# Spreading the kernel values of a long convolution: a second 0/1 matrix in place of a shifted copy, and new instruction orders

## The chip, the cores and the metric

The kernel runs on one core of one Trainium2 chip. The metric is device time in microseconds (us) of one execution; before the change it is 368.26 us, the median of three runs (367.65 to 368.64). A core has a matrix engine (TensorE, PE in the profile), a vector engine (VectorE, DVE), a scalar engine (ScalarE, ACT), GpSimd (POOL) and SyncE (SP, here used to start transfers). Each engine works through its own list of instructions in order; where one needs what another made, it waits on a semaphore.

## The reference

Two independent computations share one output of 2048 x 1280 bf16. The left half is attention with 32 heads of 20 columns, in which position s sees the eight positions s, s-2, ..., s-14. The right half is a long convolution: a kernel of 2048 taps for each of 640 channels is summed from 192 complex exponentials, and convolved with the input through Fourier transforms.

```python
idx = pos[:, None] - (jnp.arange(8) * 2)[None, :]          # left half
logits = einsum("bhsd,bhswd->bhsw", q, k[idx]) * scale      # masked where idx < 0
a = einsum("bhsw,bhswd->bhsd", softmax(logits), v[idx]) @ wo
...
l = arange(L).astype(bf16)                                  # right half: positions rounded to bf16
P = exp((dt * (A_re + 1j * A_im))[:, :, None] * l)
K = einsum("dn,dnl,dn->dl", Cc, P, dt * Bc).real            # 640 x 2048 taps
y = irfft(rfft(u, 2L) * rfft(K, 2L))[:L] + u * Dskip
```

Because the positions are rounded to bf16, the 2048 taps take far fewer distinct values: the kernel computes K for 20 offsets times 33 blocks of 8 positions, and a 0/1 matrix spreads these over the 2048 positions.

## The kernel before

**Stages.** The convolution goes through five chunks c = 0 to 4 of 128 channels. For each chunk VectorE builds two tables from powers that ScalarE made: Xtab, 20 offsets (stage xtab), and Ytab, 33 blocks (ypos for blocks 16 to 32, yneg for 0 to 15, the latter with the magnitudes of stage mag). There are two Xtab buffers, but one Ytab: ypos of the next chunk can begin only when the table products of this one have been read from Ytab. Its generators come from device memory by SyncE (taby, five transfers a chunk), and GpSimd zeroes the first block (line 546).

**Table products.** Stage kgen (two halves h of a chunk, kgen30 and kgen31 for chunk 3) multiplies the tables, channel by channel, 33 columns at a time, into two PSUM banks: 16 zeroing matmuls, 256 narrow ones with 64 rows (line 603) and 256 wide ones (line 610) for a chunk, each with its own weight load. A half was three pieces on PE: `both` (zeroing and all narrow products) and `one` twice. ScalarE then copies each bank into Kd (line 615).

**Shift and spreading.** Kd has 20 rows of each 32-row group in use. Positions that need block b + 1 where their neighbours need b take it from rows 20 to 31 of the group, into which four SyncE transfers a chunk (stage kd, line 583) copied rows 4 to 15, moved by one block. Spreading (stage spread, its first four pieces, line 635) multiplies Kd by the 0/1 matrix SEL into K; the next eight pieces are the first Fourier step of K (f1, line 656). Stage u is the same step for the input. spec is the second Fourier step (f2, line 676, copied to Sp at line 681), prod the product of both spectra on VectorE (lines 686 and 687), swap a copy of one spectrum with its halves exchanged, inv the first inverse step (ia, line 701, copied at line 704). last00 to last07 and last10 to last13 are the second inverse step, from tables HB that take the place of Xtab, Xg, krtmp and mag when those are done (stage hb, six loads). uda and udb are the input times Dskip, loaded where Xtab0 and Ytab were.

**Attention.** k0 to v3 are the projections (line 745). For each of four blocks b of 512 positions, logits has ten VectorE products (line 791), five PE pieces that sum them (line 798), then maximum, exponential and normalisation; av has ten VectorE products with v (line 840) and ten PE pieces (line 848); out is the output projection (line 865) with writes by SyncE (line 870). fetch and fetchv load q, k and v for a block. The products go through three buffers (pr), so VectorE can be at most three products ahead of PE.

**The order of work.** It is written out in lists. Every stage registers its pieces by engine (`op("P", ...)` for PE, A for ScalarE, V for VectorE, G for GpSimd, S for SyncE). TRACE lists all pieces in the order in which they are emitted, SLOTS gives the buffer of every use of the eight PSUM banks (ps) and of other shared buffers, and SEQ gives each engine's own order, which `chain` fixes by dependencies without waits:

```python
for ins in next(left[stage, engine]):
    if engine in last:
        self.tc.add_manual_dep(ins, last[engine].name, ...)
    last[engine] = ins
```

A word "kgen30.P:2" in SEQ is the next two PE pieces of stage kgen30.

## Time and profile before

| | |
|---|---|
| median of three runs | 368.26 us (367.65 to 368.64) |
| profiled execution | 368.48 us, of which the span from first to last instruction is 366.7 |
| busy: DVE, PE, ACT, POOL | 306.6, 281.9, 257.1, 35.2 us |
| mean granted PE clock | 0.900 |
| spreading, line 635 | 180 matmuls, 7.0 us busy |
| shift, line 583 | 20 issues on SP, 24 KB each, median 0.83 us |
| table products, lines 603 and 610 | 1280 matmuls each, 14.6 and 26.9 us busy |

Times in the profile are of one execution, counted from its first instruction. A row of stretches gives the stretch, its length, then for each engine the busy time with the number of instructions, then the granted share of the PE clock, the DMA engines' busy share and GB/s. In a timeline or a list of waits, "[5.51 <-PE ps_l L798]" says that the engine was idle 5.51 us before that instruction, until the named one had finished; "issue" is idle time in which it waited for nothing that the profile shows.

### The profile page before, as it was taken

What the parts mean: (1) busy time and instruction counts of PE and PEld (TensorE: products, weight loads), DVE (VectorE), ACT (ScalarE), POOL (GpSimd) and SP (SyncE); (2) the same over time, 40 slices, a digit from 0 to 9 for tenths busy, and PEclk for the clock granted to TensorE, in tenths of its full rate; (3) what the DMA queues carried; (4) which work ended last, traced back from release to release, by engine and by line L of the source; (5) the groups of instructions that cost most, each with busy time, mean ns of one, the idle gap of its engine ahead of it and who ended that gap; (6) DMA issues with size and microseconds to landing.
All of it is one profiled execution on the core that took longest, in us unless ns stands there. A gap on an engine that the chain in (4) does not pass through costs nothing.

```text
span 366.7 us, 13345 instructions
## 1 busy us (share of the span) xinstructions
PE 281.9 (77%) x5808; PEld 183.3 (50%) x5808; DVE 306.6 (84%) x397; ACT 257.1 (70%) x574; POOL 35.2 (10%) x72
## 2 busy tenths in 40 slices
PE   2429999999945787849985579869886569899983
PEld 1213434443333454637663456647565356768852
DVE  1588999999997999999999879999999259979620
ACT  3998999964530679926897048945997029999663
POOL 9550000000000000000000000000000000002282
PEclk9999999999975988958999558979999589999999
DMA  6998869897997789811739614564998689998695
GB/s 142 226 123 198 215 224 308 269 291 221 251 260 168 183 108 170 158 46 44 208 72 170 185 41 154 105 61 141 245 327 258 222 153 121 160 192 233 154 202 136
DMA packets 127114, 65.49 MB, mean 179 GB/s; under 512 B 84352, under 2 KB 123872, under 8 KB 125904
## 3 DMA queue, kind: packets, MB, share of 16 engines
q1 hardware_dynamic: 124224, 61.61, 72.7%
q0 software_dynamic: 1776, 2.79, 3.9%
q8 instruction: 45, 0.74, 0.9%
q10 hardware_dynamic: 1056, 0.25, 0.3%
q14 instruction: 13, 0.11, 0.1%
HBM read 35.25 MB, written 21.03 MB: 153 GB/s over the span
## 4 chain that ended last, share of the span: by engine, by line
PE 27%; DVE 20%; ACT 17%; issue 14%; DMA 13%; SPq 7%; ACTq 0%; DVEq 0%
PE ps_k L610 6%; ACT A L660 4%; SPq L724 4%; PE ps_k L603 4%; DVE p L840 3%; PE ps_f L676 3%; PE ps_o L848 3%; DMA out_dram<-ob 3%; ACT Sp L681 3%; PE ps_op L865 2%; DMA UT<-Sp 2%; DMA xT<-in_A_x_dram 2%; DVE prod L791 2%; ACT am L464 2%; PE ps_l L798 2%
## 5 line engine op out<-in xcount | busy, mean ns | idle before, releaser
L745 PE MATMUL ps_p<-xT,w 128*128 128x512 bf16 x300 | 68.8, 386 | 5.6 <-DMA xT<-in_A_x_dram 4.0
L791 DVE TENSOR_TENSOR prod<-qk 128x2048 bf16<-128x2048 bf16 x40 | 48.5, 1238 | 12.8 <-PE ps_l L798 12.0
L840 DVE TENSOR_TENSOR p<-vb,attn 128x2048 bf16<-128x2048 bf16 x40 | 47.5, 1225 | 10.3 <-PE ps_o L848 8.5
L745 PEld LDWEIGHTS <-w 128*128 128x128 bf16 x300 | 29.1, 98 | 44.2 <-issue 11.7
L681 ACT CAST Sp<-ps_f 128x512 bf16<-128x512 f32 (+1 forms) x96 | 44.8, 560 | 8.8 <-PE ps_f L676 8.3
L615 ACT CAST Kd<-ps_k 128x264 bf16<-128x264 f32 x20 | 7.7, 387 | 60.0 <-PE ps_k L610 60.0
L660 ACT CAST A<-ps_f 128x512 bf16<-128x512 f32 x80 | 45.7, 692 | 0.4 <-PE ps_f L656 0.4
L610 PE MATMUL ps_k<-Ytab,Xtab 128*20 128x33 bf16 x1280 | 26.9, 250 | 21.1 <-issue 21.0
L610 PEld LDWEIGHTS <-Xtab 128*20 128x20 bf16 x1280 | 23.6, 127 | 25.3 <-issue 24.7
L748 ACT CAST st<-ps_p 128x512 bf16<-128x512 f32 x60 | 31.6, 611 | 6.4 <-PE ps_p L745 4.0
L676 PE MATMUL ps_f<-A,cT 64*128 64x128 bf16 (+1 forms) x768 | 29.6, 222 | 6.1 <-issue 2.2
L676 PEld LDWEIGHTS <-cT 64*128 64x128 bf16 x768 | 22.7, 102 | 16.7 <-issue 15.6
L848 PE MATMUL ps_o<-p,cHs 64*32 64x256 bf16 x640 | 25.5, 306 | 3.3 <-DVE p L840 2.0
L556 ACT ACTIVATE mag<-ta 128x192 bf16<-128x192 f32 x80 | 24.6, 415 | 3.3 <-DVE Ytab L561 3.2
L865 PE MATMUL ps_op<-wo,oT 128*128 128x320 bf16 x160 | 24.6, 300 | 0.4 <-ACT A L660 0.4
L603 PE MATMUL ps_k<-Ytab,Xtab 64*20 64x33 bf16 x1280 | 14.6, 241 | 11.8 <-issue 11.8
L1138 POOL DMA_DIRECT2D out_dram<-ys x24 | 14.4, 608 | 95.7 <-ACT Sp L681 80.5
L546 POOL MEMSET Ytab<- 128x192 bf16 x5 | 1.3, 258 | 221.7 <-PE ps_k L610 221.7
L701 PE MATMUL ps_ia<-cE,Sp 128*128 128x128 bf16 x160 | 19.7, 219 | 2.8 <-DVE Sp L687 2.5
L509 DVE TENSOR_TENSOR krtmp<-Xtab,Xg 128x3072 bf16<-128x3072 bf16 (+1 forms) x15 | 20.5, 1368 | 0.3
L798 PE MATMUL ps_l<-prod,cGs 128*32 128x512 bf16 x160 | 17.0, 446 | 3.8 <-DVE prod L791 3.5
L603 PEld LDWEIGHTS <-Xtab 64*20 64x20 bf16 x1280 | 13.4, 120 | 12.7 <-issue 12.4
(118 smaller groups left out, 573.2 us busy)
## 6 DMA issues: line engine op xcount, KB each, us to landing
qk<-qkd SPq DMA_DIRECT2D x20, 263.0 KB
qkd<-st SPq DMA_DIRECT2D x8, 640.0 KB
UT<-Sp SPq DMA_DIRECT2D x10, 512.0 KB
Gdram<-cs SPq DMA_DIRECT2D x11, 384.0 KB
vb<-vd SPq DMA_DIRECT2D x16, 196.5 KB
Xg<-Gdram SPq DMA_DIRECT2D x4, 768.0 KB
Zdram<-Z SPq DMA_DIRECT2D x3, 1024.0 KB
zb<-Zdram SPq DMA_DIRECT2D x24, 128.0 KB
```

Of the source, the lines that this page charges most:

```text
L556: self.op("A", lambda b=b: self.nc.scalar.activation(out=self.mg[b // 8]()[:, b % 8], in_=ta()[:, s], func=ACT.Exp, scale=-16.0 * (b + 1)))
L603: MM(ps[e]()[32 * g:32 * g + 20, i, :], lhsT=X()[rows(e), :, p, col], rhs=Y()[rows(e), :, p, col], start=False, stop=False, tile_position= ...
L610: MM(ps[e]()[32 * g:32 * g + 20, i, :], lhsT=X()[:, :, p, col], rhs=Y()[:, :, p, col], start=False, stop=(p == 1), tile_position=(0, 32 * ...
L660: op("A", lambda q=q, ps=ps: nc.scalar.copy(out=A1()[:].rearrange("p k r s t -> p (k r) s t")[:, :, sig, 8 * q:8 * q + 8], in_=ps()[:]))
L676: nc.tensor.matmul(ps[h]()[:, kk], lhsT=C["T"]()[hs, k, 64 * (1 - r):64 * (1 - r) + 128], rhs=A1()[hs, k, r, s0:s1, :].rearrange("p s t -> ...
L681: op("A", lambda q=q, h=h, ps=ps: nc.scalar.copy(out=Sp()[:, slots, h, :, 4 * q:4 * q + 4], in_=ps[h]()[:].rearrange("p k (s t) -> p s t k ...
L745: nc.tensor.matmul(ps()[:], lhsT=self.w[which]()[:, kt, 128 * ct:128 * ct + 128], rhs=self.xT()[:, kt, 512 * sc:512 * sc + 512], start=(kt ...
L748: op("A", lambda ct=ct, ps=ps: nc.scalar.copy(out=st()[:, ct], in_=ps()[:]))
L791: op("V", lambda ct=ct, wg=wg, pr=pr: V.tensor_tensor(out=pr[wg]()[:], in0=self.qk[b][ct]()[:, 0, HALO:].unsqueeze(1).to_broadcast([128, 4 ...
L840: op("V", lambda t=t, qp=qp, v4=v4: V.tensor_tensor(out=v4(), in0=windows(self.v[b][t]()[:, 2 * qp:2 * qp + 2, 0:PH], 2, 4), in1=at()[:].u ...
L848: nc.tensor.matmul(ps[half]()[32 * q:32 * q + 32, t % 2], lhsT=C["Hs"]()[r], rhs=v4()[r, m, q2, :], start=(t % 2 == 0 and m == 0), stop=(m ...
L865: nc.tensor.matmul(ps()[:], lhsT=self.oT[b]()[:, t, 128 * s:128 * s + 128], rhs=self.wo_sb()[:, t, 320 * eh:320 * eh + 320], start=(t == 0 ...
```

## The change

The selection matrix is split: one part takes a position's value from its own block (rows 0 to 19), the other from the next block (rows 4 to 15 of block b + 1), read from the same Kd one block on. Where the second part is not empty, spreading adds a second matmul into the same place. The shift transfers go. The piece `both` keeps the zeroing and the first 64 of its 128 narrow products; the other 64 are a piece of their own. TRACE, SLOTS and SEQ are new as a whole, since the pieces are no longer the same.

```diff
@@ -84,10 +84,15 @@
                 assert all(np.array_equal(Wm[par], Wm[b]) for b in range(par, 8, 2))
                 per.append(Wm[par])
             if np.array_equal(per[0], per[1]):
-                ops.append((add(per[0]), bhi, None))
+                per = [(per[0], None)]
             else:
-                for par in range(2):
-                    ops.append((add(per[par]), bhi, par))
+                per = [(per[par], par) for par in range(2)]
+            for Wm, par in per:
+                here, on = np.zeros_like(Wm), np.zeros_like(Wm)
+                here[:20], on[4:16] = Wm[:20], Wm[20:]
+                ops.append((add(here), bhi, par, 0))
+                if on.any():
+                    ops.append((add(on), bhi, par, 1))
         plan.append(ops)
     return np.stack(mats, 1), plan
 
@@ -576,12 +582,6 @@
         xs(S_(8, 15, 2), S_(0, 7, 2), 4, 4)
         xs(S_(9, 16, 2), S_(0, 13, 4), 5, 4)
 
-    def shift(self):
-        nc, Kd = self.nc, self.Kd
-        for g in range(4):
-            r = 32 * g
-            self.op("S", lambda r=r: nc.sync.dma_start(out=Kd()[r + 20:r + 32, :, 0:NB - 1, :].rearrange("p h b t -> p h (b t)"), in_=Kd()[r + 4:r + 16, :, 1:NB, :].rearrange("p h b t -> p h (b t)")))
-
     def kgen(self, h):
         nc, X, Y, Kd, op = self.nc, self.X, self.Y, self.Kd, self.op
         MM = nc.tensor.matmul
@@ -595,12 +595,14 @@
             for g in range(4):
                 for e in range(2):
                     MM(ps[e]()[32 * g:32 * g + 32], lhsT=self.pools["zero"]()[rows(e)], rhs=Y()[rows(e), 0:8, 0, z0:z0 + NB], start=True, stop=False, tile_position=(64 * e, 32 * g), skip_group_check=True)
-            for p in range(2):
-                for i in range(8):
-                    for g in range(4):
-                        for e in range(2):
-                            col = narrow(g, i)
-                            MM(ps[e]()[32 * g:32 * g + 20, i, :], lhsT=X()[rows(e), :, p, col], rhs=Y()[rows(e), :, p, col], start=False, stop=False, tile_position=(64 * e, 32 * g), skip_group_check=True)
+            part(0)
+
+        def part(p):
+            for i in range(8):
+                for g in range(4):
+                    for e in range(2):
+                        col = narrow(g, i)
+                        MM(ps[e]()[32 * g:32 * g + 20, i, :], lhsT=X()[rows(e), :, p, col], rhs=Y()[rows(e), :, p, col], start=False, stop=False, tile_position=(64 * e, 32 * g), skip_group_check=True)
 
         def one(e):
             for p in range(2):
@@ -610,6 +612,7 @@
                         MM(ps[e]()[32 * g:32 * g + 20, i, :], lhsT=X()[:, :, p, col], rhs=Y()[:, :, p, col], start=False, stop=(p == 1), tile_position=(0, 32 * g), skip_group_check=True)
 
         op("P", both)
+        op("P", lambda: part(1))
         for e in range(2):
             op("P", lambda e=e: one(e))
             op("A", lambda e=e: nc.scalar.copy(out=Kd()[:, h, :, 8 * e:8 * e + 8], in_=ps[e]()[:].rearrange("p t b -> p b t")))
@@ -625,9 +628,9 @@
         def work(jp=jp, ps=ps):
             for j2 in range(2):
                 seen = set()
-                for wi, bhi, par in sorted(plan[2 * jp + j2], key=lambda o: (o[2] or 0, o[1])):
+                for wi, bhi, par, on in sorted(plan[2 * jp + j2], key=lambda o: (o[3], o[2] or 0, o[1])):
                     r = slice(32 * bhi, 32 * bhi + 32)
-                    b0 = 8 * bhi
+                    b0 = 8 * bhi + on
                     if par is None:
                         o, k = ps()[r, j2], Kd()[:, :, b0:b0 + 8, :]
                     else:
@@ -1017,7 +1020,6 @@
         op.fill(f"yneg{c}", t.yneg)
         for h in range(2):
             op.fill(f"kgen{c}{h}", t.kgen, h)
-        op.fill(f"kd{c}", t.shift)
 
     def attention_pool():
         pp.release()
...
@@ TRACE, SLOTS and SEQ are replaced as a whole; of SEQ, PE's list from chunk 1 to chunk 4:
...
-av0.P spread0.P spec0.P:4 kgen10.P kgen11.P kgen10.P:2 av0.P kgen11.P:2 av0.P u2.P spec0.P:2 av0.P u2.P spec0.P:2 out0.P:4 u2.P spread1.P out0.P:2
-u2.P spread1.P:2 out0.P spread1.P out0.P inv0.P spread1.P inv0.P logits2.P spread1.P:7 inv0.P:4 u2.P:4 inv0.P:2 av1.P:2 spec1.P:2 av1.P spec1.P
-kgen20.P:3 logits2.P kgen21.P:3 av1.P:2 spec1.P:2 av1.P spec1.P av1.P spec1.P av1.P spec1.P u3.P:8 spread2.P:4 av1.P:2 spread2.P:8 out1.P:4 kgen30.P
-inv1.P kgen31.P:3 logits2.P kgen30.P:2 inv1.P:5 logits2.P out1.P:2 inv1.P:2 u4.P spec2.P:2 out1.P logits2.P spec2.P out1.P spec2.P:2 logits2.P spec2.P
-logits2.P:2 spec2.P:2 u4.P:3 spread3.P:4 u4.P:4 logits2.P inv2.P:4 spread3.P:4 inv2.P:3 spread3.P inv2.P spread3.P:3 kgen41.P:2 logits3.P kgen40.P:2
-av2.P logits3.P kgen40.P kgen41.P spec3.P logits3.P spec3.P:2 av2.P spec3.P logits3.P spec3.P:2 av2.P spec3.P av2.P spec3.P av2.P:2 spread4.P:4
...
+logits0.P spec.P logits0.P spec.P logits0.P spec.P:5 spread0.P:8 kgen10.P u1.P:4 kgen10.P av0.P:2 u1.P:2 av0.P kgen10.P av0.P u1.P av0.P kgen10.P
+av0.P u1.P logits1.P kgen11.P av0.P kgen11.P av0.P kgen11.P logits1.P av0.P spec0.P:2 av0.P logits1.P kgen11.P spec0.P:4 spread1.P out0.P spec0.P:2
+out0.P logits1.P out0.P:2 spread1.P:3 u2.P:2 out0.P:3 inv0.P spread1.P out0.P inv0.P:7 u2.P spread1.P:7 u2.P:5 logits2.P kgen20.P kgen21.P:2
+kgen20.P:2 av1.P kgen20.P kgen21.P spec1.P kgen21.P spec1.P av1.P spec1.P av1.P spec1.P av1.P spec1.P spread2.P:4 av1.P:2 spec1.P:2 av1.P spec1.P
+av1.P u3.P:8 spread2.P:5 inv1.P:8 av1.P:2 spread2.P:3 out1.P:6 logits2.P out1.P:2 kgen30.P:2 spec2.P kgen31.P:2 kgen30.P:2 kgen31.P:2 spec2.P:5
+spread3.P:4 spec2.P:2 u4.P:8 spread3.P:8 logits3.P kgen40.P kgen41.P logits2.P kgen40.P:2 logits2.P inv2.P kgen41.P kgen40.P logits2.P kgen41.P
+logits3.P kgen41.P inv2.P logits2.P inv2.P:2 logits2.P logits3.P logits2.P inv2.P spread4.P inv2.P logits2.P logits3.P inv2.P:2 spread4.P:2 logits3.P
...
@@ of SEQ, VectorE's list around chunks 3 and 4:
...
-xtab4.V yneg3.V xtab4.V yneg3.V prod1.V:2 xtab4.V logits2.V xtab4.V logits2.V xtab4.V:2 prod1.V xtab4.V:5 logits2.V xtab4.V:3 logits2.V xtab4.V:4
-logits2.V xtab4.V:4 logits2.V xtab4.V logits2.V xtab4.V ypos4.V logits2.V ypos4.V:5 yneg4.V ypos4.V:2 prod2.V:2 ypos4.V:2 prod2.V:2 yneg4.V logits3.V
-yneg4.V logits3.V:2 logits2.V logits3.V av2.V:2 logits3.V:5 av2.V:6 prod3.V av2.V:2 prod3.V:3 logits3.V udb.V:2 logits3.V:3 uda.V:2 prod4.V:4
...
+yneg3.V ypos3.V logits2.V ypos3.V:2 xtab4.V yneg3.V xtab4.V:2 yneg3.V xtab4.V logits2.V xtab4.V:2 logits3.V xtab4.V:2 logits3.V xtab4.V:16 ypos4.V:8
+yneg4.V ypos4.V:2 yneg4.V logits2.V yneg4.V logits2.V:3 prod2.V:4 logits2.V logits3.V:2 logits2.V logits3.V logits2.V logits3.V logits2.V logits3.V:4
...
@@ of SEQ, SyncE's list around the loads of HB:
...
-hb.S kd3.S:3 taby4.S:4 hb.S swap2.S kd3.S swap2.S inv1.S hb.S taby4.S fetch3.S out1.S fetch3.S:2 hb.S:3 swap3.S:2 fetch3.S inv2.S fetch3.S out1.S:2
...
+fetchv2.S:4 taby3.S:2 fetchv2.S u4.S:4 fetchv2.S:3 fetch2.S out1.S:2 swap2.S:2 fetch2.S inv1.S taby4.S:5 hb.S out1.S:2 hb.S:5 fetch3.S:4 udb.S:3 uda.S
...
```

More of the change, by code (lines that the diff above doesn't have):

```diff
@@ L202 @@
-spread3.P u4.A spread3.P spread3.A spread3.P u4.A spread3.P ypos4.V spec2.A u4.P spread3.A u4.P u4.A u4.P prod2.V u4.A u4.P u4.A logits2.P prod2.V
-fetch3.S u4.A spread3.A logits2.A ypos4.V inv2.P spec2.A logits2.A ypos4.V spread3.A inv2.P out1.S inv2.A prod2.V inv2.P inv2.A fetch3.S prod2.V
-fetch3.S inv2.P inv2.A spread3.P:2 inv2.A spread3.P yneg4.V spread3.P spread3.A inv2.P spread3.A inv2.P hb.S inv2.A inv2.P hb.S out1.A spread3.P
-logits3.V inv2.P hb.S out1.A spread3.A spread3.P:2 spread3.A spread3.P yneg4.V inv2.A:2 logits3.V kgen41.P spread3.A inv2.A swap3.S logits3.V
@@ L280 @@
[L280 removed]
+prep.P:2 weights.P:2 prep.P weights.P:2 prep.P weights.P:3 k0.P:5 weights.P q0.P:5 q2.P:2 v0.P v2.P v0.P:4 k1.P:2 q1.P:2 k1.P:3 v2.P q1.P:3 q2.P:3
+v2.P:3 v1.P:5 q3.P:3 v3.P k3.P:2 k2.P:2 k3.P q3.P:2 k3.P:2 k2.P logits0.P k2.P v3.P logits0.P:2 k2.P v3.P logits1.P v3.P:2 kgen01.P:2 logits1.P
+kgen01.P:2 logits0.P kgen00.P:2 logits0.P kgen00.P:2 logits1.P spread0.P:2 u0.P:2 logits1.P u0.P:5 logits1.P u0.P logits0.P spread0.P:2 spec.P
```

260 lines of the change are left out of this document (131 added, 129 removed).

## The prediction

> **What bounds the kernel now.** I read the head of the profile page first, then the busy time by stretches, then the waits, then the timelines of single engines, and last the chain that ended last. Chunk and stage names are those of the order lists (kgen = the table products of L597 to L615).
>
> ```profile
> span 366.7 us, 13345 instructions
> ...
> PE 281.9 (77%) x5808; PEld 183.3 (50%) x5808; DVE 306.6 (84%) x397; ACT 257.1 (70%) x574; POOL 35.2 (10%) x72
> ...
> q8 instruction: 45, 0.74, 0.9%
> ```
>
> No engine is full: DVE, the busiest, idles 60.1 us of 366.7. Where it idles shows in the stretches. I cut the span at the first and last table product of each chunk (rows 1 to 5), after the last of them (row 6), and at the last negation of the Y table of chunk 4, which ends at 279.8 (rows 7 and 8).
>
> ```profile
> core 0: us, PE busy (x) PEld busy (x) DVE busy (x) ACT busy (x) POOL busy (x), PEclk, DMA share, GB/s
> 101.00:121.00 20.00, 10.28 (x547) 8.22 (x547) 17.08 (x24) 4.25 (x12) 0.00 (x0) 0.66 0.94 202
> 153.60:168.10 14.50, 9.24 (x549) 7.78 (x552) 13.98 (x20) 5.81 (x15) 0.00 (x0) 0.65 0.21 61
> 196.70:215.90 19.20, 9.87 (x542) 7.81 (x544) 16.57 (x23) 4.27 (x13) 0.00 (x0) 0.62 0.58 136
> 236.90:250.70 13.80, 9.58 (x547) 8.30 (x547) 13.48 (x19) 6.15 (x22) 0.00 (x0) 0.75 0.46 55
> 279.10:297.50 18.40, 11.10 (x564) 8.39 (x565) 10.28 (x9) 4.83 (x10) 0.00 (x0) 0.72 0.74 220
> 297.50:360.80 63.30, 57.54 (x1131) 42.66 (x1130) 43.15 (x38) 50.56 (x114) 13.88 (x24) 0.97 0.93 173
> 0.00:279.80 279.80, 213.70 (x4125) 132.41 (x4125) 253.92 (x352) 200.95 (x448) 20.74 (x48) 0.90 0.76 179
> 279.80:350.30 70.50, 59.35 (x1587) 44.63 (x1581) 52.70 (x47) 49.32 (x111) 6.21 (x11) 0.90 0.87 179
> ```
>
> In the five kgen stretches (85.9 us together) PE is busy 50.1 us, ACT 25.3 us, at a granted clock of 0.62 to 0.75. After them PE is busy 57.5 of 63.3 us at 0.97: the end is set by work on PE. Inside kgen the time goes here:
>
> ```profile
> PEld L610 <- issue: 24.7, 18, 5.5
> PE ps_k L610 <- issue: 21.0, 9, 5.3
> ...
> DVE prod L791 <- PE ps_l L798: 12.0, 4, 5.5
> PE ps_k L603 <- issue: 11.8, 5, 3.9
> ```
>
> PE stands 21.0 + 11.8 = 32.8 us before its own table products with nothing to wait for but its instructions. The page's queue row says what this is: 45 instruction packets for 11,616 matmuls and weight loads, so one brings about 258. A chunk's kgen is 528 matmuls and 528 loads, 4.1 packets, and executes only about 9 us:
>
> ```profile
> 279.10:297.50 18.40, 8.89 (x528) 1.29 (x3) 0.72 0.74 220
> ```
>
> (This row counts only what writes ps_k.) The stretches last 13.8 to 20.0 us all the same, 3.4 to 4.9 us a packet. The Trainium skill, "Runtime: NRT & Kernel Launch", section "Instruction fetch mechanics", has refills of 16 KiB, 256 instructions, and calls their cost mostly hidden; the size agrees with the 258, the hiding does not agree with the 32.8 us. Other PE work needs fewer packets per microsecond, so kgen mixed with it would cost less.
>
> Who pays for it is DVE: in chunk 4 it waits three times for logits whose matmuls stand behind kgen pieces on PE.
>
> ```profile
> 288.80 1.23 DVE L791 TENSOR_TENSOR prod<-qk 128x2048 bf16<-128x2048 bf16 x1 [5.51 <-PE ps_l L798]
> ...
> 293.59 1.23 DVE L840 TENSOR_TENSOR p<-vb,attn 128x2048 bf16<-128x2048 bf16 x1 [2.42 <-PE ps_o L848]
> ...
> 300.84 2.36 DVE L791 TENSOR_TENSOR prod<-qk 128x2048 bf16<-128x2048 bf16 x2 [3.53 <-PE ps_l L798]
> ```
>
> **The change, part by part.** *The transfer that goes.* Twenty issues leave SP, four a chunk:
>
> ```profile
> 122.07 2.70 SPq L583 DMA_DIRECT2D Kd<-Kd  x3
> 124.89 1.42 SPq L542 DMA_DIRECT2D Ytab<-Gdram  x3
> ```
>
> That is 0.9 us each, 18 us of SP in all. On the path they stood only where something waited behind them, as here, ahead of the Y generators of chunk 1: up to 2.7 us, and that Y table was then not the next thing DVE needed (it had logits left). Spreading itself was queued behind other PE work, in chunk 4 from 297.5 until 310.1, so its wait for the copy was covered. I take 0 for the missing transfer itself; 2.7 us is the upper end.
>
> *The second matrix.* Worked out from the selection code, spreading goes from 36 matmuls a chunk to 52, 80 more in all; SEL grows from 72 to 96 KB on POOL's load queue, which nobody needs before spread0.
>
> ```profile
> 310.13 1.06 PE L635 MATMUL ps_s<-Kd,cSEL 128*32 128x256 bf16 x36
> ```
>
> 16 more at 1.06/36 = 0.029 us is 0.47 us a chunk, 2.4 us in all; only the last (0.5 us) lies in the stretch that PE fills.
>
> *kgen in four pieces instead of three.* No instruction is added; the 64 narrow products of the second half become a piece of their own, between which logits and others can stand.
>
> *The orders.* These move far more than the rest. By the two PE lists: the products of chunk 1 now have 8 u1, 10 av0, 3 logits1 and 2 spec0 pieces between them (before: one av0); those of chunk 2 one av1 and one spec1, of chunk 3 one spec2, of chunk 4 three logits2, one logits3 and one inv2 piece. All of inv1 and out1 now come before kgen of chunk 3 (before: 4 out1 pieces and no inv1); all of inv2 after the first products of chunk 4 (before: ahead of them). SP's list keeps its loads; all six HB loads now come after the last Y generators, swap3 behind loads that wait for the end of chunk 4's kgen, the last of the eight fetchv3 behind output writes of last00. POOL's list is the same in substance. The cover for these: prod3, which needs swap3, comes some 30 us after kgen; the last fetchv3 is needed by the fifth av3 product, and if late costs at most a landing, which for an output write at the end takes 4.87 us (below).
>
> *The start of kgen 3.* Ahead of the last negation of chunk 3, DVE has 3 products of prod1 and one xtab4 more and one logits2 less:
>
> ```profile
> L791 DVE TENSOR_TENSOR prod<-qk 128x2048 bf16<-128x2048 bf16 x40 | 48.5, 1238 | 12.8 <-PE ps_l L798 12.0 <-PE ps_o L848 0.4 <-DMA qk<-qkd 0.4
> L840 DVE TENSOR_TENSOR p<-vb,attn 128x2048 bf16<-128x2048 bf16 x40 | 47.5, 1225 | 10.3 <-PE ps_o L848 8.5 <-PE ps_l L798 1.8
> ```
>
> Full-size products of this kind take 1.24 us, about 1.2 back to back: +2.7 us. Against it, chunk 2's kgen held DVE up here, and with a finer order I count 3 us as saved:
>
> ```profile
> 216.99 2.36 DVE L840 TENSOR_TENSOR p<-vb,attn 128x2048 bf16<-128x2048 bf16 x2 [1.71 <-PE ps_o L848]
> 219.80 0.56 DVE L509 TENSOR_TENSOR krtmp<-Ytab 128x768 bf16<-128x768 bf16 x1 [0.45 <-DMA Ytab<-Gdram]
> ```
>
> So kgen 3 starts at about 237, as before. The second row gives another price: from the end of kgen (215.9) to the first step of the next Y table it is 3.9 us (zeroing, generator load, landing).
>
> *From kgen 3 to kgen 4.* With little between its pieces kgen 3 takes 13.8 (as it did, at a DMA share of 0.46) to 19.2 us (chunk 2); I take 15.5, since the orders leave the load about as it was: end at 252.5, Y table free for DVE at 256.4. What DVE has to do meanwhile, and then up to kgen 4, comes from how it fills those stretches now:
>
> ```profile
> 237.30:261.30 24.00, 19.25 (x692) 15.28 (x677) 23.54 (x33) 14.82 (x38) 0.45 (x2) 0.86 0.59 130
> 215.90:236.90 21.00, 19.28 (x298) 12.75 (x296) 19.02 (x21) 18.93 (x42) 0.45 (x2) 0.86 0.47 121
> 261.30:279.80 18.50, 15.05 (x222) 11.32 (x221) 18.11 (x21) 17.78 (x38) 0.00 (x0) 1.00 0.91 294
> ```
>
> From the end of yneg3 to ypos4 (first row) it loses three prod1, six steps of logits2 and one of xtab4 and gains two products of logits3: 23.5 less about 7 is 16.5 us, until 253.5. So it idles 3 us. From ypos4 to the end of yneg4 (third row) four prod2 and a short logits2 step go, 5.2 us of 18.5: 13 us are left, and kgen 4 starts at 269, 10 us earlier than the 279.1 of now. As a check: 4 prod2 and 7 steps of logits2 less and one logits3 more ahead of it are 9 to 10 us of DVE.
>
> *kgen 4 and the end.* The same 528 products with a few small pieces: 18.4 to 19 us, end at 288. From there to the end it is 366.7 - 297.5 = 69.2 us now, and what was moved behind kgen comes on top: 7 inv2, 4 logits2 and one av2 piece and the 0.5 us of spreading.
>
> ```profile
> L701 PE MATMUL ps_ia<-cE,Sp 128*128 128x128 bf16 x32 | 3.8, 220 | 0.5 <-DVE Sp L687 0.4
> ```
>
> This row is eight inv pieces of chunk 3 (the UT half overlaps it): 0.48 us each, so 3.4; the logits pieces an estimated 1.4, av 0.6: 5.9 us of PE. The stretch has 63.3 - 57.5 = 5.8 us of PE idle, so between 0 and 5.9 us appear; PE being the full engine, I take 5.
>
> ```profile
> 353.73 2.47 PE ps_op L865 x19
> 356.20 4.87 DMA out_dram<-ob
> ```
>
> The last output write stays as it is.
>
> **Sum.** 288 + 69.2 + 5 = 362.2 us of span. The profiled execution took 368.48 for its 366.7, so 1.8 lie around: 364.0, which is 4.5 below that execution and 4.3 below the median of 368.26. (DVE alone would end sooner: 269 + 52.7 + 9.5 of busy time + some 10 idle + the 16.4 us after its last step = 358.) About 0.3%, 1.1 us, is what a measurement of this kernel can tell from no change.
>
> **Rivals.** *A. Chunk 3 turns into the wait (slower).* Between kgen 2 and kgen 3 (215.9 to 236.9, where PE, DVE and ACT are all busy 19 of 21 us) now come 8 inv1, 4 more out1 and some spec1 pieces more, and DVE is left only 16.5 us of work to cover kgen 3, where it had 23.5. If ACT's evacuations hold kgen 3 back by 4 us and it takes chunk 2's 19.2 us, it ends at 260.2, ypos4 starts at 264.1, kgen 4 at 277, and the sum is 277 + 19 + 74.2 + 1.8 = 372. The point that decides: kgen 3 ending after about 257 gives the whole gain back. For it: two of five kgen stretches are over 19 us. Against: chunk 3's was the shortest. *B. Instructions arrive in time (faster).* If pieces stand finely enough for the packets to be fetched behind other work, kgen 4 lasts 13.8 us and the moved work fills idle PE: 269 + 13.8 + 69.2 + 1.8 = 354. By the Trainium skill's sentence above on hidden refills this would be the rule. Against: within kgen 4 only five pieces stand, which need instructions as well. *C. It all cancels.* The transfer was hidden, and what DVE wins before kgen 4 comes back as work after it: 9 to 10 us of DVE moved for 9 to 10 us earlier: 367.2 to 369.4. *D. New order, new collisions:* HB and fetch3 loads beside kgen 4, or the late fetchv3: 2 to 6 us on the forecast, 366 to 370, and with A up to 375.
>
> **How the numbers follow.** Forecast 0.38, B 0.08, C 0.10, A 0.28, D 0.16; of D 0.11 is slower, 0.03 within the bound and 0.02 faster. Faster is 0.38 + 0.08 + 0.02 = 0.48, same 0.10 + 0.03 = 0.13, slower 0.28 + 0.11 = 0.39. The range runs from close to B to A and most of D: 355 to 375; the forecast's own, with kgen 3 from 13.8 to 17 us and 0 to 5.9 us at the end, 359 to 366.
>
> **What would show it.** Right: no L583 rows, 260 spreading matmuls, kgen 4 starting near 269 and ending near 288, the "issue" waits of PE still there, DVE waiting under 6 us in kgen 4 (11.5 now), PE over 90% busy after it. Wrong: kgen 3 ending after 257 with DVE idle for over 7 us before ypos4 (A), kgen stretches near 14 us throughout (B), or kgen 4 earlier by 9 us and the stretch after it longer by as much (C).

## The result, and the profile after

The changed kernel takes 369.82 us (median of 20 executions, 367.46 to 373.71), the kernel before beside it 368.19 (20 executions): a ratio of 1.0058, 95% interval 1.0029 to 1.0086. It is slower by about half a per cent; 364.0 had been forecast. (Comparisons leave out executions that are more than 1.5% above the fastest of the same kernel; where the ratio so found and that of the medians differ by more than 0.25%, both are given.)

The profiled execution took 367.46 us, the shortest of the 20, so two more executions of the changed kernel were profiled (373.93 and 370.67 us); they are called the second and the third profile. From the page of the first:

```profile
span 365.6 us, 13461 instructions
...
PE 286.7 (78%) x5888; PEld 185.4 (51%) x5888; DVE 307.1 (84%) x397; ACT 256.7 (70%) x574; POOL 35.1 (10%) x72
...
q8 instruction: 46, 0.75, 0.9%
```

The same five stretches between the first and last table product of a chunk, and the stretch from there to the last matmul:

```profile
110.00:127.20 17.20, 10.05 (x556) 7.87 (x556) 17.10 (x22) 2.32 (x5) 0.00 (x0) 0.81 0.82 193
144.70:169.20 24.50, 20.10 (x757) 14.40 (x759) 24.46 (x31) 16.39 (x43) 0.00 (x0) 0.86 0.57 98
194.10:209.30 15.20, 9.77 (x562) 8.02 (x564) 14.93 (x22) 5.89 (x18) 0.00 (x0) 0.66 0.57 84
238.50:255.30 16.80, 8.66 (x547) 7.86 (x548) 16.59 (x23) 5.07 (x16) 0.00 (x0) 0.65 0.44 130
271.60:287.30 15.70, 12.47 (x569) 9.37 (x569) 15.63 (x15) 3.87 (x8) 0.00 (x0) 0.89 0.32 93
287.30:357.40 70.10, 64.94 (x1227) 47.73 (x1226) 48.03 (x45) 55.79 (x125) 13.38 (x23) 0.98 0.96 190
```

Chunk 4's products run from 271.6 to 287.3, where 269 to 288 was forecast and 279.1 to 297.5 was before. But chunk 0's begin at 110.0, 9 us later than the 101.0 of before, and from 287.3 to the span's end it is 78.3 us, where 69.2 was before. TensorE waits less for the instructions of the table products than before (32.8 us), and VectorE less for logits (12.0; 11.0 and 8.2 in the second and third profile). In a list of waits the three numbers are the total in us, how many waits, and the longest:

```profile
PE ps_k L605 <- issue: 14.1, 6, 4.6
...
PE ps_k L612 <- issue: 8.7, 5, 3.0
DVE prod L794 <- PE ps_l L801: 7.9, 4, 4.9
...
ACT st L751 <- DMA qkd<-st: 7.0, 1, 7.0
```

The last line, ScalarE's wait until a store has left its buffer, read before the change:

```profile
ACT st L748 <- DMA qkd<-st: 1.9, 1, 1.9
```

It is the first hint of where the gain went.

**VectorE's idle time as the ledger.** VectorE does the same 397 instructions in both kernels, 306.6 and 307.1 us, so the difference of two spans is the difference of its idle time. Cut at five of its own steps (first logits product, first step of the Y table of chunks 1 and 4, first product of prod3, end), idle time is the length of the stretch (the number behind it) less its DVE busy time. Before:

```profile
core 0: us, PE busy (x) PEld busy (x) DVE busy (x) ACT busy (x) POOL busy (x), PEclk, DMA share, GB/s
0.00:81.00 81.00, 60.67 (x320) 27.51 (x321) 65.26 (x125) 69.83 (x138) 18.93 (x40) 1.00 0.93 220
81.00:130.50 49.50, 36.04 (x736) 18.76 (x735) 46.21 (x56) 22.06 (x51) 0.45 (x2) 0.86 0.88 213
130.50:261.30 130.80, 101.92 (x2861) 74.83 (x2857) 124.34 (x155) 91.28 (x223) 1.36 (x6) 0.83 0.58 124
261.30:311.70 50.40, 37.52 (x1050) 27.29 (x1050) 38.09 (x37) 32.62 (x68) 0.00 (x0) 0.86 0.87 218
311.70:366.70 55.00, 45.74 (x859) 34.89 (x854) 32.75 (x30) 41.26 (x98) 14.42 (x24) 0.99 0.86 180
```

After:

```profile
0.00:87.70 87.70, 68.47 (x345) 30.84 (x346) 70.54 (x128) 72.40 (x145) 18.93 (x40) 0.96 0.90 207
87.70:132.50 44.80, 30.26 (x688) 15.32 (x687) 39.13 (x48) 15.66 (x36) 0.45 (x2) 0.85 0.91 223
132.50:257.90 125.40, 98.66 (x2903) 74.50 (x2903) 122.62 (x154) 93.80 (x231) 1.36 (x6) 0.88 0.62 133
257.90:310.00 52.10, 45.40 (x1178) 30.98 (x1172) 46.49 (x46) 39.19 (x81) 0.00 (x0) 0.97 0.79 184
310.00:365.60 55.60, 43.88 (x782) 33.77 (x782) 28.32 (x24) 35.68 (x86) 14.37 (x24) 0.92 0.86 192
```

| VectorE idle, us | to first logits | to Y 1 | to Y 4 | to prod3 | to the end | sum |
|---|---|---|---|---|---|---|
| before | 15.7 | 3.3 | 6.5 | 12.3 | 22.2 | 60.0 |
| changed, the profile above | 17.2 | 5.7 | 2.8 | 5.6 | 27.3 | 58.6 |
| changed, second profile | 18.7 | 9.3 | 1.8 | 7.1 | 27.4 | 64.3 |
| changed, third profile | 16.2 | 7.1 | 5.2 | 6.3 | 26.6 | 61.4 |

By the mean of three executions the change wins 3.2 + 6.0 = 9.2 us between Y 1 and prod3, the stretch that the forecast reckoned, and loses 5.8 us ahead of it (1.7 + 4.1) and 4.9 behind it; 0.8 us of VectorE work comes on top. (Without the second profile, by far the longest execution, it is 8.8 won, 4.1 and 4.7 lost.) In the first profile, the chain of waits names a wait of 8.80 us in the part ahead:

```profile
82.84 1.37 ACT st L751 x3
84.21 8.80 DMA vd<-st
...
93.09 0.59 ACT st L751
```

and SP's queue shows what was put around that store (vb are loads of the v blocks of block 0 of the positions, fetchv0 in the lists, first used by VectorE at 147.7):

```profile
80.61 1.37 SPq L761 DMA_DIRECT2D wo<-in_A_wo_dram  x2
82.17 0.45 SPq L768 DMA_DIRECT2D qk<-qkd  x1
82.67 1.44 SPq L781 DMA_DIRECT2D vb<-vd  x3
84.21 0.41 SPq L754 DMA_DIRECT2D vd<-st  x1
84.67 2.56 SPq L781 DMA_DIRECT2D vb<-vd  x2
```

### The profile page after: what moved, and what is told of

It reads as the page before. It is cut to its first block, busy times and chain, and to the rows that moved or that the text cites. A ratio compares the mean times of both kernels' runs of the same rounds, so it can differ in the third digit from the quotient of the medians.

```text
span 365.6 us, 13461 instructions
## 1 busy us (share of the span) xinstructions
PE 286.7 (78%) x5888; PEld 185.4 (51%) x5888; DVE 307.1 (84%) x397; ACT 256.7 (70%) x574; POOL 35.1 (10%) x72
## 4 chain that ended last, share of the span: by engine, by line
DVE 35%; PE 25%; issue 8%; DMA 8%; ACT 8%; SPq 2%; ACTq 0%; DVEq 0%
DVE prod L794 6%; PE ps_p L748 5%; DMA UT<-Sp 4%; DVE krtmp L515 4%; DVE Xtab L525 3%; DVE p L843 3%; PE ps_op L868 3%; DVE UT L689 3%; PE ps_o L851 3%; DVE Sp L690 3%; PE ps_k L612 3%; DMA vd<-st 2%; PE ps_ia L704 2%; DVE Ytab L567 2%; ACT Sp L684 2%
## 5 line engine op out<-in xcount | busy, mean ns | idle before, releaser
L748 PE MATMUL ps_p<-xT,w 128*128 128x512 bf16 x300 | 74.3, 409 | 12.6 <-ACT st L751 9.7
L748 PEld LDWEIGHTS <-w 128*128 128x128 bf16 x300 | 30.6, 103 | 54.9 <-issue 23.9
L663 ACT CAST A<-ps_f 128x512 bf16<-128x512 f32 x80 | 44.7, 747 | 0.6 <-PE ps_f L659 0.6
L679 PE MATMUL ps_f<-A,cT 64*128 64x128 bf16 (+1 forms) x768 | 27.9, 213 | 3.4 <-ACT K L643 0.7
L605 PE MATMUL ps_k<-Ytab,Xtab 64*20 64x33 bf16 x1280 | 15.8, 241 | 14.5 <-issue 14.1
L679 PEld LDWEIGHTS <-cT 64*128 64x128 bf16 x768 | 21.1, 97 | 11.6 <-issue 10.6
L704 PE MATMUL ps_ia<-cE,Sp 128*128 128x128 bf16 x160 | 21.6, 230 | 5.0 <-DVE Sp L690 5.0
L605 PEld LDWEIGHTS <-Xtab 64*20 64x20 bf16 x1280 | 13.7, 121 | 16.4 <-issue 15.5
L704 PE MATMUL ps_ia<-cE,UT 128*128 128x128 bf16 x160 | 21.4, 229 | 0.0
```

Of the source, the lines that this page charges most:

```text
L663: op("A", lambda q=q, ps=ps: nc.scalar.copy(out=A1()[:].rearrange("p k r s t -> p (k r) s t")[:, :, sig, 8 * q:8 * q + 8], in_=ps()[:]))
L679: nc.tensor.matmul(ps[h]()[:, kk], lhsT=C["T"]()[hs, k, 64 * (1 - r):64 * (1 - r) + 128], rhs=A1()[hs, k, r, s0:s1, :].rearrange("p s t -> ...
L704: nc.tensor.matmul(ps()[:, i], lhsT=X()[:, h, 4 * t:4 * t + 4, :].rearrange("p g k -> p (g k)"), rhs=C["E"]()[:, n_, :], start=(i == 0 and ...
L748: nc.tensor.matmul(ps()[:], lhsT=self.w[which]()[:, kt, 128 * ct:128 * ct + 128], rhs=self.xT()[:, kt, 512 * sc:512 * sc + 512], start=(kt ...
```

## The experiments

All times are medians, with the kernel before on the same chip beside them; ratios are to that.

### Is the loss ahead of chunk 0 that of the early loads?

One edit of the changed kernel, in the order lists:

```diff
-genm1.S fetchv0.S:2 fetch0.S wo.S:2 fetch0.S fetchv0.S:3 v1.S fetchv0.S:2 fetch0.S wo.S:2
+genm1.S fetch0.S wo.S:2 fetch0.S v1.S fetch0.S wo.S:2
...
-taby1.S:5 tab2.S
+taby1.S:5 fetchv0.S:7 tab2.S
```

> The changed kernel with one edit: in SP's list the seven early loads of the v blocks of chunk 0 are issued behind the fifth table store of y1 and no longer among the projection's stores; nothing else is moved. T1 (the gain of the middle is lost ahead of kernel generation 0, where the store of v's first half took 8.80 us behind those loads and the projections waited for the store buffer): kernel generation 0 begins at 101 to 104 us (110.0 in the changed kernel, 101.0 before), the last product of kernel generation 4 ends at 281 to 283 (287.3), the time is 364 to 366. T2 (the late start is absorbed: the middle waits for instructions and for transfers anyway, and what is won early comes back as work later): kernel generation 0 begins early again, but generation 4 ends within 1.5 us of 287 and the time is within 1.5 us of the changed kernel's 369.8.

Measured: 368.07 against 370.47, 0.9923 (0.9886 to 0.9959): 1.3% below the changed kernel's 1.0058, which is 4.9 us, and now faster than before. (What the expectation calls the v blocks of chunk 0 are those of block 0 of the positions.) The changed kernel once more, on the same chip:

> The changed kernel itself once more, for the spread of its stages from one execution to the next. If the losses ahead of generation 0 and at the end are those of the order and not of one execution: generation 0 begins within 2 us of 110.0, the matmuls end 7 to 9 us before the span's end, the wait for the output buffers is 4 us or more, the time is 368 to 371. If they are chance: generation 0 begins at 101 to 107 in this one.

Measured: 373.82 (367.41 to 375.95), medians 1.009, ratio 0.9977 (0.9923 to 1.0031). Its executions spread so widely that the ratios, 0.9923 and 0.9977, don't tell the two apart on this chip; the averages of all 12 executions each do, with 367.7 us for the loads late and 372.6 for the changed kernel, 4.9 us. Chunk 0's products begin at 113.8 in this execution, 3.8 us later than in the first profile and so outside what was expected, but not earlier: the late start is no chance.

The first two stretches with the loads late:

```profile
0.00:90.00 90.00, 68.82 (x345) 30.74 (x346) 70.57 (x128) 72.51 (x145) 18.73 (x40) 0.98 0.93 202
90.00:132.90 42.90, 30.89 (x693) 15.73 (x692) 39.44 (x48) 16.30 (x37) 0.45 (x2) 0.80 0.80 203
```

In the second, 42.90 - 39.44 = 3.5 us are idle, as before the change (3.3), where the changed kernel had 5.7 to 9.3. This holds for every profile taken of a kernel with the new orders: in thirteen with the loads early this stretch has 5.7 to 10.4 us of idle time, in four with the loads late 2.6 to 3.5, whatever else was edited. (The 1.7 us of the first stretch are not explained by the loads: it has 15.5 to 19.4 us idle with them late.)

T1's markers were wrong: chunk 0's products still begin at 109.5, since TensorE's new list puts them behind the first logits of block 1, and chunk 4's end at 288.1 where 281 to 283 was expected. The first profile was too lucky a yardstick; in the second, on the same chip, they end at 292.6. The start of chunk 0 was no measure of the loss; VectorE's idle time was. T2's condition, an early start, did not come about, and the time did fall.

The old order has five of these loads ahead of late stores too, but behind those of q2 and q3. Put further forward in the kernel before:

```diff
-wo.S fetch0.S:3 v2.S tab1.S q2.S fetch0.S q3.S fetchv0.S fetch0.S fetchv0.S:4 fetch1.S:2
+wo.S fetch0.S:3 v2.S fetchv0.S:5 tab1.S q2.S fetch0.S q3.S fetch0.S fetch1.S:2
```

> The kernel before with one edit: five of its loads of chunk 0's v blocks are issued behind the second store of v, ahead of the projection's last stores, where the remade order has such loads. T1 (loads ahead of the projection's stores fill the queues, ScalarE waits for its two store buffers, the logits come late and VectorE idles, whatever the rest of the order): VectorE's idle time between the first logits product and the first ypos1 rises from 3.3 us by 2 to 6 us and the time by as much, 1.005 to 1.016 of the kernel before. Rival (it needs the remade order of the projections too): within 0.3% of the kernel before.

Measured: 376.02 against 370.64, 1.0133 (1.0083 to 1.0182).

```profile
81.50:137.20 55.70, 36.77 (x752) 19.11 (x753) 46.33 (x56) 21.90 (x53) 0.45 (x2) 0.88 0.87 195
```

The second stretch has 9.4 us of idle time, 6.1 more than before. The cause is shown from both sides: taken out of the new order the early loads give 1.3%, put into the old one they cost 1.3%.

### Through what do the loads cost?

The store could stand behind the loads in SP's list, or share full DMA engines with them, or matter only because ScalarE has two store buffers.

```diff
+        e, queue = ("A", nc.scalar) if (which, sc) in (("v", 1), ("q", 3), ("k", 3), ("k", 2), ("v", 3)) else ("S", nc.sync)
-            op("S", lambda: nc.sync.dma_start(
+            op(e, lambda: queue.dma_start(
```

> The changed kernel with the last five stores of the projections issued by ScalarE's own queue, behind the copies that fill their buffer, instead of SP's; the early v loads stay where they are. Theory Q (the stores are late because they stand behind the loads in one list and one queue): their landing falls from 9 to 12 us to under 5, ScalarE's waits for its store buffers are under 2 us, the time is 3 to 6 us below the changed kernel's. Theory B (the 16 DMA engines are full in this stretch, share 0.9 or more, and a store shares them whoever issues it): landing 6 us or more, the waits stay over 4 us, within 2 us of the changed kernel.

Measured: 371.49 against 369.59, 1.0065 (1.0027 to 1.0102), as the changed kernel. The landing of these stores (last number, us; between 74 and 108 us) in the changed kernel and here:

```profile
qkd<-st SPq DMA_DIRECT2D x3, 640.0 KB, 9.0
```

```profile
qkd<-st ACTq DMA_DIRECT2D x3, 640.0 KB, 9.3
```

Theory B holds: another queue changes nothing, and ScalarE still waits 8.4 us for its store buffers (76 to 116 us). The Trainium skill, "Trainium Kernel Development and Optimization", Quick Reference, Key Constraints, says that the queues of SP, ACT and POOL all run on the same 16 DMA engines and that issuing from several saves issue time alone; the 9.0 and 9.3 us agree with that. With the loads late, the three stores of q and k in this window landed after 6.4 us (the two of v after 7.4, where the changed kernel has 6.8):

```profile
qkd<-st SPq DMA_DIRECT2D x3, 640.0 KB, 6.4
```

```diff
-        st = lazy(lambda: op.slot(self.pools["xw"], "st", 2, [128, 5, 512], bf16, "st"))
+        st = lazy(lambda: op.slot(self.pools["xw"], "st", 3, [128, 5, 512], bf16, "st"))
```

> The changed kernel with a third buffer between the projections and their stores, nothing else. If the late start is ScalarE's wait for one of two store buffers: that wait goes from 9 us to under 2, VectorE's idle time between the first logits product and the first ypos1 falls from 5.6 to 9.9 us to 3.5 to 5, the time is 3 to 5 us below the changed kernel's. Rival (the logits need what the late stores write, so the wait only passes from the buffer to the load of q and k): the wait goes, VectorE's idle time there and the time stay within 1.5 us.

Measured: 371.16 against 369.59, 1.0054 (1.0020 to 1.0087). ScalarE's wait for the store goes from 7.0 to 1.0 us, and this stands in its place (76 to 116 us):

```profile
PE ps_l L801 <- DVE prod L794: 5.9, 4, 2.5
...
DVE prod L794 <- DMA qk<-qkd: 3.7, 2, 2.8
```

In the changed kernel the first of these lines has 1.1 us there, and the second does not occur. The rival was right: the logits need what the late stores write, so the wait passes on to the loads of q and k, and VectorE's idle time in the second stretch is still 6.0 us. What is left for the early loads to take is transfer time, in a stretch at a DMA share of 0.91.

### The end

> The changed kernel with one edit: the third and fourth output copies of the last chunk go to two q/k tiles that are dead by then, so that no copy waits until an earlier output write has left its buffer. T1 (part of the loss at the end is ScalarE's wait of 4.8 and 1.1 us for the two output buffers): ScalarE's wait for them is under 1 us, from the last matmul to the end it is 5 to 6 us instead of 8.2, the time is 3 to 4 us below the changed kernel's. Rival (the output writes themselves set the end, the queues being busy): the wait goes, the last write still lands when it did, the time is within 1 us of the changed kernel's.

```diff
-            ob = lazy(lambda: op.slot(self.pools["att"], "ob", 2, [128, D], bf16, "ob"))
+            if b == 3 and s > 1:
+                ob = lazy(lambda s=s: self.pools["att"].tile([128, D], bf16, name="ob", tag=f"qk{s - 2}", bufs=1))
+            else:
+                ob = lazy(lambda: op.slot(self.pools["att"], "ob", 2, [128, D], bf16, "ob"))
```

Measured: 372.48 against 370.47, 1.0040 (1.0006 to 1.0075): no gain to be seen. The wait for output buffers falls (first the changed kernel, then this one), and from the last matmul to the end it is 7.9 us instead of 8.2:

```profile
ACT ob L871 <- DMA out_dram<-ob: 5.9, 2, 4.8
```

```profile
ACT ob L874 <- DMA out_dram<-ob: 1.2, 2, 1.0
```

The rival holds; the wait was a symptom. Next, swap3 ahead of uda on SP, alone and with the loads late:

```diff
-udb.S:3 uda.S swap3.S uda.S:2 swap3.S inv2.S
+udb.S:3 swap3.S:2 uda.S:3 inv2.S
```

> The changed kernel with one edit: in SP's list the two transfers of swap3 stand ahead of the three of uda instead of between them. T1 (swap3 sets the end: in the changed kernel prod3 waited 2.7 us for its landing, and swap4, prod4 and the last inverses follow from prod3): prod3 begins 2 to 3 us earlier against the last output product of chunk 1 on VectorE, its wait is under 0.5 us, the time is 2 to 3 us below that of the changed kernel. Rival (the end is set by the queues of the output writes): the wait goes and the time stays within 1 us.

Measured: 373.08 against 370.64, medians 1.007, ratio 0.9979 (0.9930 to 1.0029); the changed kernel, measured again on another chip, had 1.009 and 0.9977. VectorE's idle time in the stretch that ends at prod3 falls to 2.9 us (5.6 to 7.1 in the changed kernel) and rises behind it to 29.9 (26.6 to 27.4).

> The changed kernel with both edits of order in SP's list: the seven early v loads behind y1's table stores, and swap3 ahead of uda. T1: the two add up, as they lie in different stretches of a VectorE that has nearly no idle time between: 7 to 8 us below the changed kernel, 0.980 to 0.988 of the kernel before. Rival (the second edit's gain is absorbed by the output writes): as with the first alone, 0.992 of the kernel before.

Measured: 366.68 against 370.64, 0.9865 (0.9815 to 0.9915), medians 0.989; the interval overlaps that of the loads alone. In the changed kernel, and with both edits:

```profile
DVE UT L689 <- DMA UT<-Sp: 3.1, 2, 2.7
```

```profile
DVE late L1113 <- DMA late<-in_B_u_dram: 2.2, 1, 2.2
```

The wait before prod3 goes, so VectorE comes to udb's product some 4 us sooner (at 311.0 instead of 315.2) and waits there for udb's last load, which SP issues no sooner than before: from prod3 to prod4 it took 17.3 us in the changed kernel and 19.8 with both edits. This part of T1 falls; a gain of the second edit is not shown.

> The two edits of order together, and at the end the third and fourth output buffer of the last chunk in tiles that are dead by then, with their two output writes issued by ScalarE's queue instead of SP's. T1 (the end is SP's queue, where eight issues of output writes took 6.8 us in the run with spare buffers alone): from the last matmul to the end 5 to 6 us instead of 8, the time 2 to 3 us below that of the two edits alone. Rival (the transfers themselves are the limit, whoever issues them): within 1 us of the two edits alone.

(Edits: the two above, the spare buffers, and `nc.scalar.dma_start` for their two writes.) Measured: 367.25 against 370.64, 0.9843 (0.9782 to 0.9904), medians 0.991; from the last matmul (352.7) to the span's end (361.1) it is 8.4 us. Nothing is won over the two edits, and the queue that issues is again not the limit.

> All edits that may help in one: the v loads late, swap3 first, spare output buffers with their writes on ScalarE's queue, and three store buffers for the projections. T1: 0.975 to 0.984 of the kernel before, as the third buffer takes what is left of ScalarE's wait (3.2 us in the run with the v loads late). Rival (with the v loads late the buffers no longer hold anything up): 0.984 to 0.988, as without the third buffer.

Measured: 366.22 against 369.59, 0.9928 (0.9893 to 0.9963). By medians the four versions with the loads late lie between 0.989 and 0.994; they beat both kernels, and nothing among them beyond that one edit is shown to help. VectorE's 4.9 us behind prod3 stay open beyond the work that the forecast had moved there: no edit here took them away.

### The second matrix

The kernel before, with its orders and three pieces, and only the matrix in place of the transfer:

```diff
-                ops.append((add(Wm), bhi, par))
+                here, on = np.zeros_like(Wm), np.zeros_like(Wm)
+                here[:20], on[4:16] = Wm[:20], Wm[20:]
...
-        op.fill(f"kd{c}", t.shift)
```

> The kernel before with only the second 0/1 matrix: spreading reads the unshifted kernel values, the shifting transfers are gone; the orders and the three-piece table products stay those of before. T1 (the transfer is hidden by the distance between generation and spreading, the forecast's term of 0 to -2.7 us, against 0.5 to 2.4 us for the added matmuls): 367 to 369 where the kernel before has 368.2. T3 (the shifting transfer stands in the path): 365 or less. T3b (the added matmuls cost more than the forecast has): 371 or more.

Measured: 372.84 against 370.47, 1.0070 (1.0033 to 1.0106), 2.4 us by medians, between T1 (up to 0.8 us more) and T3b (2.8 or more): the forecast's price for all the matmuls (2.4) with 0 for the transfer. That would settle it, but leaving the added products out of the new order,

```diff
                 for wi, bhi, par, on in sorted(plan[2 * jp + j2], key=lambda o: (o[3], o[2] or 0, o[1])):
+                    if on:
+                        continue
```

> The changed kernel without the products with the second 0/1 matrix: the 20 added spreading matmuls of each chunk are left out (the kernel values that come from a neighbouring block are missing from the result). Its time is read for what the added matmuls cost in the new order. By the forecast's term (0.47 us a chunk on TensorE): 2.4 us below the changed kernel. By the run with the matrix alone in the old order: 2 to 3 us below. Rival (TensorE has idle time to take them): within 0.7 us.

gave 378.09 against 369.59, 1.0251 (1.0193 to 1.0309): not faster, but 1.9% slower than the changed kernel (1.0058). (They are 80, 16 a chunk, by the 5,888 and 5,808 matmuls of the two pages; the 20 in the expectation was a slip.) Neither theory has room for that. What 80 matmuls fewer also do is shift every later border between TensorE's instruction packets, by 32 instructions a chunk of the 256 or so in a packet. So the stages were left alone and the borders were moved, with narrow matmuls ahead of the first projection:

```diff
+                if which == "k" and sc == 0 and ct == 0:
+                    for _ in range(32):
+                        nc.tensor.matmul(ps()[:, 0:8], lhsT=self.w[which]()[:, 0, 0:128], rhs=self.xT()[:, 0, 0:8], start=True, stop=True, skip_group_check=True)
```

> The changed kernel with 32 narrow matmuls (8 columns) added to TensorE ahead of the first k projection, into a bank that the projection then overwrites: 64 instructions more, so that every later instruction packet of TensorE begins a quarter of a packet earlier in the program. Theory P (where the packets' borders fall among the stages is worth several us): more than 2 us off the changed kernel in either direction. Theory C (only the work counts): within 1.5 us of it (some 1 us of TensorE at about 30 us, where it isn't the bound).

Measured: 379.00 against 366.57, 1.0332 (1.0265 to 1.0398).

> The same with 64 narrow matmuls, half a packet. Theory P: more than 2 us off the changed kernel or off the run with 32. Theory C: within 2 us of the changed kernel.

Measured: 377.05 against 366.57, 1.0307 (1.0252 to 1.0361).

> The changed kernel with 128 narrow matmuls at the start, 256 instructions: a whole packet (0.75 MB in 46 packets is 16.3 KB each), so the borders among the later stages lie where they lay in the changed kernel, while the added matmuls themselves cost twice what they cost with 64. Theory P: within 1% of the changed kernel (some 3 us of TensorE at about 21 us, partly covered), so 1.005 to 1.015 of the kernel before, far below the 1.033 and 1.031 with a quarter and half a packet. Rival (the added matmuls cost by themselves, by delaying the projections): 1.035 or more.

Measured: 373.53 against 367.44, 1.0168 (1.0126 to 1.0210), with the changed kernel on the same chip at 370.42, 1.0067 (1.0031 to 1.0103):

> The changed kernel itself, beside the run with a whole packet on the same chip: 1.003 to 1.010 of the kernel before.

A whole packet of padding costs 1.0%, a little more than Theory P had; a quarter of these matmuls costs 2.7%. If all of the 1.0% is the added matmuls' own cost and it goes with their number, 2.4% of the run with 32 is left for something else, and 1.9% of the run with 64 (3.1 - 0.7 - 0.5). The work added does not explain it, and the place of the borders would. With 32, TensorE stands 4.6 us at 120.5, ahead of logits products that VectorE needs at once, with nothing to wait for but instructions:

```profile
DVE prod L797 <- PE ps_l L804: 14.0, 7, 4.6
...
PE ps_l L804 <- issue: 5.7, 2, 4.6
```

(VectorE's wait was 7.9 to 11.0 us in the three profiles of the changed kernel.) With the whole packet, TensorE waits again where it waited in the changed kernel:

```profile
PE ps_k L605 <- issue: 12.7, 6, 4.3
...
PE ps_k L612 <- issue: 7.1, 5, 3.0
```

> The changed kernel with each of the 80 added spreading matmuls (16 a chunk; the run without them spoke of 20) issued twice, which doubles the suspected cost (their values count twice in the result). Theory C, by the forecast's price of 0.029 us a matmul: 1 to 2.4 us above the changed kernel. Theory P: anything from 5 us below to 5 us above, as the 160 instructions more move the borders.

```diff
+                    for again in range(1 + on):
```

Measured: 374.63 against 366.57, 1.0225 (1.0172 to 1.0277): 1.6% or 5.8 us above the changed kernel (1.0067), which is more than either theory had allowed for 80 matmuls more.

> The kernel without the added spreading matmuls, which was 1.025 of the kernel before, with the 64 narrow matmuls at the start. Theory P: it leaves the 1.025 by 1% or more, as its packets begin half a packet off. Theory C, or another cause that lies in the missing products themselves: 1.02 to 1.03 again.

Measured: 373.35 against 366.57, 1.0114 (1.0042 to 1.0186), medians 1.0185. With 64 matmuls more than the run without the products it is 1.4% faster by the ratio, 0.5% by the medians (1.0185 against 1.0230), so it decides little: Theory P's per cent is there by one measure and not by the other.

So much is shown: 32 or 64 idle matmuls ahead of the first projection cost this kernel more than 128 do, so the cost does not go with the work added (by ratios to the kernel before; the changed kernel itself was not measured on the chip of the runs with 32 and 64). That it is the packets' borders is not shown. TensorE's matmuls wait 25.5 to 26.4 us for instructions in the three profiles of the changed kernel, 29.4 with 32 matmuls, but 25.0 with 64 and 23.7 with 128; 27.5 without the products, and 30.4 without them and with 64. These totals don't follow the times. Only for the run with 32 does a trace show one long wait at a place that VectorE needs; for 64 and for the missing products the way to the loss is open.

What the 80 products cost as work cannot be read off any of these runs; the +0.7% of the matrix alone and the +1.9% of leaving it out both lie within what idle matmuls do. The change itself also adds 160 instructions to TensorE's list and reorders it, so some of its own 0.6% may be of this kind. The experiments on the loads and on the end don't suffer from it: their TensorE lists are the same, instruction for instruction, as those of the kernel they are compared with.

## Why the prediction was wrong, step by step

In the terms of the forecast's sum, with all three profiles of the changed kernel (us; the last column is the span):

| | kgen 3 starts | kgen 4 starts | kgen 4 lasts | from there to the end | span |
|---|---|---|---|---|---|
| forecast | 237 | 269 | 19 | 74.2 | 362.2 |
| first profile | 238.5 | 271.6 | 15.7 | 78.3 | 365.6 |
| second | 244.5 | 277.0 | 15.6 | 79.5 | 372.1 |
| third | 240.1 | 274.7 | 15.9 | 78.3 | 368.9 |

- **The gain before kgen 4: right.** From the first step of the Y table of chunk 1 to kgen 4 it was 148.6 us before, and 139.1, 138.4 and 141.6 after: 7 to 10 us are won, as the steps of VectorE's list had it (ypos4 to kgen 4 in the first profile 13.7 us, forecast 12.6, before 17.8). That kgen 4 ends at 287.3 where 288 was forecast is luck: it starts 2.6 us late and lasts 3.3 less than taken. Rival A did not happen: kgen 3 ends at 255.3, 260.3 and 258.4, past its 257 in two profiles, but because everything ahead was late; VectorE idles at most 5.2 us in the whole stretch before ypos4. Nor did Rival B (kgen stretches of 15.2 to 24.5 us in the first profile).
- **"SP's list keeps its loads", and so kgen 3 "as before": the first step that failed.** The list does keep its loads, but the prediction looked at where they stand only from kgen 1 on. Ahead of kgen 0, loads that VectorE uses some 65 us later were put before a projection's store, in a stretch at a DMA share of 0.9. That term was taken as nothing, and kgen 3 starts 1.6 to 7.6 us late. By the runs the loads cost 1.3%, 4.9 us, and without them the same change is at 0.9923 of before, about 365.4 on the 368.26 of the forecast's base, where 364.0 had been forecast. Kgen 4's short length hides part of this in the sum.
- **"I take 5" for the work behind kgen: the second, wrong in every profile.** From kgen 4's end to the span's end it became 9.1 to 10.3 us longer. In the first profile TensorE has 64.9 - 57.5 = 7.4 us more work there, where 5.9 was reckoned; its idle time until the last matmul shrinks by 0.6 (5.8 to 5.2), where 0.9 was reckoned; and "the last output write stays as it is" was wrong by 2.3 (8.2 us after the last matmul, 8.1 and 7.0 in the other two, against 5.9). The three add up to the 9.1. Why the last writes end later is open: neither spare buffers (7.9) nor another queue (8.4) brought it back.
- **swap3 and the last fetchv3: the covers held only in part.** VectorE waited 2.7 us for swap3 and 2.5 us for a v block (3.4 and 2.7 in the other profiles); the first wait, once removed, came back as one for udb's load.
- **The transfer at 0 and the matrix at 0.5 us of its 2.4: not settled**, for the reason above; the matrix alone in the old order came out 2.4 us slower.
- **Rival C** comes out near the measured time, but not by its mechanism alone: of the 9.2 us won, 4.9 came back as idle time behind prod3; the rest of the loss lay ahead of kgen 0. **Rival D** (new collisions, 366 to 370) had the kind and the size right, but not the place: beside kgen 4 the DMA share was only 0.32, and the late fetchv3 cost 2.5 to 3.4 us.

## What to carry to other kernels

When a change remakes an issue order, compare the whole list of the DMA queue, from the first load, not only the stages that the change is about: in a stretch where the DMA engines are full, a load that nobody needs yet delays the stores that everybody needs, from either of the two queues tried here and with two buffers or three. On a kernel whose busiest engine always does the same work, cut its idle time at its own steps: that ledger found both losses at once, while the start of a stage was no measure of either. Take more than one profile of each kernel: the first one here met a forecast by luck. Before a per cent is put down to a few matmuls more or less, add idle ones at the start; if that moves the time as much, the per cent cannot be put down to the work of those matmuls.

## What was not expected of the hardware

- Sixty-four instructions more on TensorE, beside 11,776, made the kernel 2.7% slower, 256 more only 1.0%; why is not shown.
- The Trainium skill, "Runtime: NRT & Kernel Launch", section "Instruction fetch mechanics", calls the crossing of a block of 256 instructions mostly hidden; the 22.8 us that TensorE's table products still wait with nothing to wait for but instructions, in the changed kernel, don't agree.
- Eighty matmuls fewer made the kernel 1.9% slower.
- Stores of 640 KB landed after 9.0 us from SP's queue and after 9.3 from ScalarE's.
- In chunk 4's stretch the granted clock was 0.89 with other work mixed in (0.89 and 0.79 in the other profiles, 0.72 before), and 0.65 in chunk 3's (0.71 and 0.61), which has one other piece in it.
